# A long-convolution and gated-FFN kernel: the down projection is interleaved with the last iterations of the main loop

## The chip, the cores and the metric

The kernel runs on one core of a Trainium2 chip. The metric is the device time of one execution in microseconds. Before the change four runs took 963.98 to 967.84 us, median 966.01.

## The reference

The input `A_u` holds 2048 tokens with 576 channels. Each token is normalized. Three terms are added: the input, a state-space convolution of the normalized input, and a gated feed-forward network (FFN) of it.

```
xn = layernorm(u)                                   # 2048 x 576
K[d, l] = Re( sum_n C[d,n] * exp(dt[d]*A[d,n]*l) * dt[d]*B[d,n] )   # N = 128 states
y[l, d] = sum_{m<=l} K[d, l-m] * xn[m, d] + xn[l, d] * Dskip[d]
h       = relu(xn @ W_gate) * (xn @ W_up)           # 2048 x 4608
out     = u + y + h @ W_down
```

The FFN takes its input from the same normalized tokens; `B_x` is not read by the sum. The reference takes the convolution by FFT; the kernel computes it in blocks.

## The kernel before, in words

Each engine (PE, DVE, ACT, GpSimd, SP) has a list of instructions written out by one Python program, in program order. An engine runs its list strictly in that order; `wait` puts a wait for a semaphore count into it. All DMAs are issued by SP, so a wait in SP's list holds every DMA that is written after it.

After a setup (parameters, layer norm, transposed input `xnT`, reversed input `xnUr`), the main loop runs over iterations i = 0 to `NITER`. The 576 channels are taken four at a time, as 144 groups `sg` (`SGN`). The 2048 tokens are 16 chunks of 128. For a group the work is:

- G: powers of the state matrix, from a broadcast DMA of `muG` (L633), ACT's exponential and two sines (L651, L662, L663) and a DVE product (L677). This is done four to eight groups ahead, four groups in a block.
- R: eight matmuls of G with the reversed input (L693, L694), iteration i = sg. DVE copies the result (L711).
- E: eight transposes of G (L793) and a copy to a slot of `Ept` (L799); there are `NE` = `DY` + 1 slots.
- A scan over the 16 chunks on GpSimd, for eight groups at once (a batch, 18 in all): a memset (L730), 15 steps of three dependent operations (L738, L740, L742), then the products that make the right-hand sides of the cross term, ending with L774. It is written into GpSimd's list after the batch's last R.
- The cross term, which carries the state into each chunk, `DY` iterations after R (L833, L834): it needs E and the scan of its batch. DVE adds it to `xyev`, which gathers the output in SBUF (L845), and keeps a column of the convolution kernel K (L846).
- For each `KG` channels the K columns are transposed (L855), copied (L863) and written to DRAM by SP (`Kpad`, L866). From there a DMA builds Toeplitz matrices for two groups (L882), in one of three slots, and their matmuls (L898) come `DT` iterations after R. DVE adds the result to `xyev` (L908).

The FFN is cut into 288 units (128 hidden features by 256 tokens). A unit is ten matmuls (L976), a maximum (L989) and a product (L993) on DVE. SP stores two units of hidden states at a time to `hT_scr` in DRAM (L1017), from four slots; L993 of a unit waits for the store that frees its slot. `_ffn_w` gives a weight to each iteration, and the share of the weights up to i is the share of units that are out by then. Weight slabs come by DMA (L942, L945) for each 16 units.

At i = `SGN` + 10 SP waits for the last scan, among others, and loads all of W_down in four DMAs (L1063) over dead buffers. After the loop a second phase follows. SP waits for everything, then loads hidden states in blocks of 256 tokens, two slots (L1195). For each chunk of 128 tokens PE runs 36 pairs of matmuls (L1224, L1226). DVE adds the projection and the input (L1234, L1235) and then `xyev` (L1237) into a staging buffer, which SP stores (L1239) as soon as it is done.

In the order of one iteration, PE's list has R, the FFN units, the cross term, the K transpose, the E transposes and the Toeplitz matmuls; DVE's has the FFN steps, the copy of E, then the results of R, cross, K and Toeplitz.

Of the kernel before, what the change touches and what calls it, by code (L numbers as in the profile page):

```python
# [6 lines left out]
dt = mybir.dt  # L7
ACT = mybir.ActivationFunctionType
ALU = mybir.AluOpType

P = 128
# [116 lines left out]
def bass_parallel_sum__ssm_conv_s4__glu_gated_reglu__prompt_kernel(  # L128
# [16 lines left out]
    ctx = ExitStack()  # L145
    ctx.__enter__()

    L = A_u.shape[1]
    D = A_u.shape[2]
    N = A_A_re.shape[1]  # L150
    F = B_W_gate.shape[1]
    C = L // P
    KT = (D + P - 1) // P
    DR = [min(P, D - P * k) for k in range(KT)]
    FT = F // P
    assert L % P == 0 and N == P and F % 512 == 0 and D % 4 == 0 and D > 512

    SGN = D // 4
# [3 lines left out]
    NBATCH = D // SB  # L162
# [5 lines left out]
    NGM = BK + 2  # L168
    NT = 3
    NH = 4  # L170
    DY = 20
    NE = DY + 1
    KG = 32
    SG_PER_KG = KG // 4
    NKG = D // KG
    DT = DY + SG_PER_KG + 4
# [5 lines left out]
    NUNITS = NFB * FT_PER_FB * NTB  # L182
# [9 lines left out]
    sp = Eng("sync")  # L192
    act = Eng("scalar")
    pe = Eng("tensor")
    dve = Eng("vector")
# [85 lines left out]
    def Eslot(sg):  # L281
        t = Ept[sg % NE]
        return {"all": t, "r": t[:, 0, :, :], "i": t[:, 1, :, :]}
    Rsb = [A.tensor([SB, 2, C], dt.bfloat16) for _ in range(2)]
    Hst1 = A.tensor([SB, 2, C], dt.float32)
    Hst = [Hst1, Hst1]
# [20 lines left out]
    ph1_top = A.top  # L307

    A.top = ph0_base
    TB2 = 256  # L310
    NTB2 = L // TB2
    wd = A.tensor([FT, D], dt.bfloat16)
    assert A.top <= early_dead_top, (A.top, early_dead_top)
    hblk = [A.tensor([FT, TB2], dt.bfloat16) for _ in range(2)]
    xst = [A.tensor([D], dt.bfloat16) for _ in range(2)]
    acc32 = [A.tensor([D], dt.float32) for _ in range(2)]
    ost = [A.tensor([D], dt.bfloat16) for _ in range(2)]
    ph2_top = A.top
    print(f"[kern] arena: persistent={persistent_top} ph0_top={ph0_top} ph1_top={ph1_top} ph2_top={ph2_top} of {A.nbytes}")

# [517 lines left out]
    def emit_ycev(sg, bank, base, yg):  # L838
        d0, k, p0, r32 = sg_info(sg)
        dve.wait(tYCpe[sg], tokYevInit, ygrp["last_pe"][yg])  # L840
        pv = psf(bank, base, 68)
        in_y = bass.AP(tensor=pv.tensor, offset=pv.offset, ap=[pv.ap[0], [1, C], [17, 4]])
        out_y = xyev[:, :, d0:d0 + 4]
        in_k = bass.AP(tensor=pv.tensor, offset=pv.offset + C, ap=[pv.ap[0], [17, 4]])
        dve.op(lambda e: e.tensor_tensor(out_y, in_y, out_y, ALU.add), g_dve)  # L845
        tKcol[sg] = dve.op(lambda e: e.tensor_copy(Kall[:, d0:d0 + 4], in_k), g_dve)  # L846
        tYCev[sg] = tKcol[sg]
# [54 lines left out]
    def emit_yiev(sg, bank, base, yg):  # L902
        d0, k, p0, r32 = sg_info(sg)
        dve.wait(tYIpe[sg], tYCev[sg], ygrp["last_pe"][yg])
        pv = psf(bank, base, 64)
        in_y = bass.AP(tensor=pv.tensor, offset=pv.offset, ap=[pv.ap[0], [1, C], [C, 4]])
        out_y = xyev[:, :, d0:d0 + 4]
        tYIev[sg] = dve.op(lambda e: e.tensor_tensor(out_y, in_y, out_y, ALU.add), g_dve)  # L908

    def emit_ygroup_evacs(yg):  # L910
# [90 lines left out]
    def emit_hdma(u):  # L1001
# [18 lines left out]
        else:  # L1020
# [3 lines left out]
            if u2 is not None:  # L1024
# [3 lines left out]
                dst2 = hT_dram[ft2, :, TB * tb2:TB * tb2 + TB]  # L1028
                tHdma[u2] = sp.op(lambda e: e.dma_start(dst2, hst[u2 % NH][:, :]), g_hdma[u2 % NH], 16)

    def _ffn_w(i):
        if i < 40:
            return 1.35
        if i < SGN:
            return 1.0
        return 0.55
    _wtot = sum(_ffn_w(i) for i in range(NITER + 1))
    _wcum = []
    _acc = 0.0
# [9 lines left out]
    g_wd = [S(f"g_wd{q}") for q in range(4)]  # L1049
    tWd = []  # L1050

    def emit_wd_prefetch():
        sp.wait(tEcp[SGN - 1], tEtr[SGN - 1], tRev[SGN - 1], tZ[NBATCH - 1], tScan[NBATCH - 1],
                tGprod[SGN - 1], tGact[SGN - 1], tGmag[SGN - 1], tRpe[SGN - 1])
        for gi_ in range(NGB):
            sig = g_gbc[gi_]
            sp.wait((sig, sig.count))
        FT_PER = 9
        assert FT % FT_PER == 0
        for q in range(FT // FT_PER):  # L1060
            src = bass.AP(tensor=B_W_down.tensor, offset=B_W_down.offset + q * FT_PER * P * D,
                          ap=[[D, P], [P * D, FT_PER], [1, D]])
            tWd.append(sp.op(lambda e, q=q, src=src: e.dma_start(wd[:, FT_PER * q:FT_PER * (q + 1), :], src), g_wd[q], 16))  # L1063

    def emit_iteration_body(i):
        if i == SGN + 10:
            emit_wd_prefetch()
        if i < SGN:
            emit_R(i, i)
        target_units = int(round(NUNITS * _wcum[min(i, NITER)]))  # L1070
# [76 lines left out]
    assert len(tYIev) == SGN and len(tYCev) == SGN, (len(tYIev), len(tYCev))  # L1147
    assert len(tHdma) == NUNITS

    tokYev = tYIev[SGN - 1]  # L1150
    tokH = [tHdma[u] for u in range(NUNITS - NH, NUNITS)]
    tokPh1PE = tYIpe[SGN - 1]
    tokPh1PEf = tFFpe[NUNITS - 1]

    if STOP_AFTER == "phase1":
        finish_debug_phase1(locals())
        return

    emit_phase2(locals())


def emit_phase2(v):
    nc = v["nc"]
    sp, act, pe, dve, pool = v["sp"], v["act"], v["pe"], v["dve"], v["pool"]
    S = v["S"]
    P_, D, C, L, FT, KT, DR = P, v["D"], v["C"], v["L"], v["FT"], v["KT"], v["DR"]
    g_pe, g_dve, g_act = v["g_pe"], v["g_dve"], v["g_act"]
    psf = v["psf"]
    wd, hblk, xst, acc32, ost = v["wd"], v["hblk"], v["xst"], v["acc32"], v["ost"]
    hT_dram, B_W_down, x_pcd, out_pcd = v["hT_dram"], v["B_W_down"], v["x_pcd"], v["out_pcd"]  # L1170
    xyev = v["xyev"]
    TB2, NTB2 = v["TB2"], v["NTB2"]
    tHdma, NUNITS, NH = v["tHdma"], v["NUNITS"], v["NH"]
    tokYev, tokPh1PE, tokPh1PEf = v["tokYev"], v["tokPh1PE"], v["tokPh1PEf"]
    tFFev, tFFpe = v["tFFev"], v["tFFpe"]
    g_hdma = v["g_hdma"]

    tWd = v["tWd"]
    assert len(tWd) == 4, "wd prefetch not emitted"
    g_hb = [S("g_hb0"), S("g_hb1")]  # L1180
    g_xs = [S("g_xs0"), S("g_xs1")]
    g_out = [S("g_out0"), S("g_out1")]

    pe_last = tokPh1PE
    sp.wait(tokPh1PE, tokPh1PEf, tokYev, (v["g_act"], v["g_act"].count), (v["g_pool"], v["g_pool"].count),
            (g_dve, g_dve.count))
    for u in range(max(0, NUNITS - NH), NUNITS):
        sp.wait(tHdma[u])
    for s_ in range(NH):
        sig = g_hdma[s_]  # L1190
        sp.wait((sig, sig.count))
    def load_hblk(tb):
        s = tb % 2
        src = bass.AP(tensor=hT_dram, offset=TB2 * tb, ap=[[L, P], [P * L, FT], [1, TB2]])
        return sp.op(lambda e: e.dma_start(hblk[s][:, :, :], src), g_hb[s], 16)  # L1195

    def load_x(c):
        s = c % 2
        return sp.op(lambda e: e.dma_start(xst[s][:, :], x_pcd[:, c, :]), g_xs[s], 16)

    tHb = {}
    tXs = {}
    tHb[0] = load_hblk(0)
    if NTB2 > 1:
        tHb[1] = load_hblk(1)
    tXs[0] = load_x(0)
    tXs[1] = load_x(1)
    tDown = {}
    tComb = {}
    tOut = {}  # L1210
    B_D = [(0, 1), (2, 3)]
    pe.wait(*tWd)
    for tb in range(NTB2):
        s = tb % 2
        pe.wait(tHb[tb])
        for tt in range(TB2 // P):
            c = (TB2 // P) * tb + tt
            par = c % 2
            bA, bB = B_D[par]
            if c - 2 >= 0:  # L1220
                pe.wait(tComb[c - 2])
            for f in range(FT):
                lhsT = hblk[s][:, f, P * tt:P * tt + P]
                pe.op(lambda e, bA=bA, lhsT=lhsT, f=f: e.matmul(psf(bA, 0, 512), lhsT, wd[:, f, 0:512],  # L1224
                                                             start=(f == 0), stop=(f == FT - 1)), g_pe)
                t = pe.op(lambda e, bB=bB, lhsT=lhsT, f=f: e.matmul(psf(bB, 0, D - 512), lhsT, wd[:, f, 512:D],  # L1226
                                                                 start=(f == 0), stop=(f == FT - 1)), g_pe)
            tDown[c] = t
            ss = c % 2
            dve.wait(tDown[c], tXs[c], tokYev)  # L1230
            if c - 2 >= 0:
                dve.wait(tOut[c - 2])
            a32 = acc32[ss]
            ta = dve.op(lambda e, a32=a32, bA=bA, ss=ss: e.tensor_tensor(a32[:, 0:512], psf(bA, 0, 512), xst[ss][:, 0:512], ALU.add), g_dve)  # L1234
            tb_ = dve.op(lambda e, a32=a32, bB=bB, ss=ss: e.tensor_tensor(a32[:, 512:D], psf(bB, 0, D - 512), xst[ss][:, 512:D], ALU.add), g_dve)  # L1235
            dve.wait(ta, tb_)
            tComb[c] = dve.op(lambda e, a32=a32, ss=ss, c=c: e.tensor_tensor(ost[ss][:, :], a32[:, :], xyev[:, c, :], ALU.add), g_dve)  # L1237
            sp.wait(tComb[c])
            tOut[c] = sp.op(lambda e, c=c, ss=ss: e.dma_start(out_pcd[:, c, :], ost[ss][:, :]), g_out[ss], 16)  # L1239
            if c + 2 < C:  # L1240
                sp.wait(tComb[c])
                tXs[c + 2] = load_x(c + 2)
        if tb + 2 < NTB2:
            sp.wait(tDown[(TB2 // P) * tb + (TB2 // P) - 1])
            tHb[tb + 2] = load_hblk(tb + 2)
    finish(v["nc"], v["ctx"], [sp, act, pe, dve, pool], [(g, g.count) for g in g_out])


def finish(nc, ctx, engs, final_waits):
# [86 lines left out]
```

## Time and profile before

| | |
|---|---|
| median of four runs | 966.01 us |
| profiled execution, its own time | 965.23 us |
| its span, first to last instruction | 963.4 us |
| mean granted TensorE clock | 0.901 |
| PE busy | 676.2 us (70%) |
| DVE busy | 592.6 us (62%) |
| GpSimd busy | 498.1 us (52%) |
| ACT busy | 425.1 us (44%) |
| first R copy, last R copy | 156.2 us, 718.3 us |
| first scan, last scan begin | 182.2 us, 730.6 us |
| first matmul of the second phase | 816.1 us |

Busy shares are averages over stages with different limits: the second phase has PE alone, the main loop has all five engines. The small gaps between GpSimd's dependent steps are not counted as busy, though nothing else can run in them.

### The profile page before, as it was taken

To read this page: it belongs to the slowest core of one execution; us is meant where nothing else is said; L and a number is where in the kernel's file an instruction comes from. 1 tells how busy PE (TensorE), PEld (TensorE's weight loads), DVE (VectorE), ACT (ScalarE), POOL (GpSimd) and SP (SyncE) were. 2 spreads that over 40 slices of the span, in tenths; PEclk is the share of its full clock that TensorE was granted. 3 is DMA by queue.
4 is the path that set the end of the run, shared out by engine and by line. 5 is a ranking of instruction groups with operands and counts; after the bars stand their busy time and mean duration, and the time that the engine had idled before them with its cause. 6 is when DMAs were issued, how large, how long until landed. Compare 5 with 4: busy or idle time off the path is not lost.

```text
span 963.4 us, 21136 instructions
## 1 busy us (share of the span) xinstructions
PE 676.2 (70%) x8215; PEld 536.1 (56%) x8215; DVE 592.6 (62%) x1656; ACT 425.1 (44%) x602; POOL 498.1 (52%) x1004
## 2 busy tenths in 40 slices
PE   0040407887977967887878977887795164999998
PEld 0020306776866856776767866776684153555554
DVE  1639956886967967887878887888584042111111
ACT  0420149875846767678776767768400000000000
POOL 0000000388878788888888888888888400000000
PEclk9999967999989878988989887999898577999999
DMA  4000033544355455456665566464442467474760
GB/s 141 13 0 0 1 100 102 157 112 136 84 158 157 117 163 145 139 137 162 155 153 154 130 164 169 106 163 116 129 105 62 154 178 195 127 193 126 196 174 25
DMA packets 192195, 120.37 MB, mean 125 GB/s; under 512 B 86176, under 2 KB 173664, under 8 KB 192096
## 3 DMA queue, kind: packets, MB, share of 16 engines
q1 hardware_dynamic: 192096, 119.03, 46.6%
q8 instruction: 65, 1.06, 0.4%
q14 instruction: 34, 0.28, 0.1%
HBM read 97.17 MB, written 21.82 MB: 124 GB/s over the span
## 4 chain that ended last, share of the span: by engine, by line
PE 34%; DVE 20%; POOL 18%; DMA 15%; issue 5%; ACT 5%; SPq 4%; POOLq 0%; DVEq 0%; ACTq 0%
PE ps_all L976 14%; PE ps_all L1224 13%; DMA hT_scr<-arena 8%; POOL arena L738 5%; POOL arena L742 4%; DMA arena<-muG 3%; POOL arena L740 3%; DVE arena L799 3%; DVE arena L989 2%; DVE arena L993 2%; DVE arena L499 2%; DVE arena L677 2%; PE ps_all L793 2%; PE ps_all L1226 2%; DVE arena L528 2%
## 5 line engine op out<-in xcount | busy, mean ns | idle before, releaser
L976 PE MATMUL ps_all<-arena 128*128 128x256 bf16 x2880 | 381.7, 292 | 6.0 <-DVE arena L993 6.0
L976 PEld LDWEIGHTS ps_all<-arena 128*128 128x128 bf16 x2880 | 286.1, 104 | 53.6 <-DVE arena L993 6.5
L993 DVE TENSOR_TENSOR arena<-arena,ps_all 128x256 bf16<-128x256 bf16 x288 | 121.3, 421 | 110.9 <-DMA hT_scr<-arena 101.8
L651 ACT ACTIVATE arena<-arena 128x512 bf16<-128x512 bf16 x144 | 95.8, 714 | 156.4 <-DMA arena<-muG 140.7
L738 POOL TENSOR_TENSOR arena<-arena 128x128 f32<-128x128 f32 x270 | 145.5, 539 | 21.2
L1224 PE MATMUL ps_all<-arena 128*128 128x512 bf16 x576 | 143.3, 384 | 13.1 <-DMA arena<-hT_scr 13.1
L989 DVE TENSOR_SCALAR arena<-ps_all 128x256 bf16<-128x256 f32 x288 | 120.2, 418 | 29.2 <-PE ps_all L976 28.2
L693 PE MATMUL ps_all<-arena 128*128 128x16 bf16 x576 | 46.5, 170 | 106.2 <-DVE arena L908 64.7
L742 POOL TENSOR_TENSOR arena<-arena 128x64 f32<-128x64 f32 x270 | 106.0, 393 | 21.1
L662 ACT ACTIVATE arena<-arena 128x512 bf16<-128x512 bf16 x144 | 115.7, 803 | 0.5
L663 ACT ACTIVATE arena<-arena 128x512 bf16<-128x512 bf16 x144 | 115.2, 800 | 0.0
L1226 PE MATMUL ps_all<-arena 128*128 128x64 bf16 x576 | 111.6, 194 | 0.0
L740 POOL TENSOR_TENSOR arena<-arena 128x64 f32<-128x64 f32 x270 | 100.0, 370 | 21.2
L677 DVE TENSOR_TENSOR arena<-arena 128x2048 bf16<-128x2048 bf16 x72 | 97.5, 1354 | 17.2 <-ACT arena L663 17.2
L1224 PEld LDWEIGHTS ps_all<-arena 128*128 128x128 bf16 x576 | 56.7, 98 | 83.0 <-issue 15.9
L799 DVE COPY arena<-ps_all 128x1024 bf16<-128x1024 bf16 x144 | 98.5, 684 | 0.8 <-PE ps_all L898 0.7
L693 PEld LDWEIGHTS ps_all<-arena 128*128 128x128 bf16 x576 | 36.7, 97 | 110.1 <-DVE arena L908 67.5
L793 PE MATMUL ps_all<-arena 128*128 128x128 bf16 x1152 | 92.0, 225 | 0.0
L1234 DVE TENSOR_TENSOR arena<-ps_all,arena 128x512 f32<-128x512 f32 x16 | 11.1, 692 | 130.3 <-PE ps_all L1226 130.3
L793 PEld LDWEIGHTS ps_all<-arena 128*128 128x128 bf16 x1152 | 70.5, 100 | 1.6
L555 POOL MEMSET arena<- 128x32 bf16 x4 | 1.0, 418 | 130.5 <-DVE arena L528 130.5
L833 PE MATMUL ps_all<-arena 128*128 128x17 bf16 x576 | 47.6, 173 | 22.9 <-POOL arena L774 22.9
(111 smaller groups left out, 896.0 us busy)
## 6 DMA issues: line engine op xcount, KB each, us to landing
arena<-muG SPq DMA_DIRECT2D x72, 512.0 KB, 6.6
hT_scr<-arena SPq DMA_DIRECT2D x144, 128.0 KB, 2.7
arena<-Kpad SPq DMA_DIRECT2D x72, 256.0 KB, 4.9
arena<-hT_scr SPq DMA_DIRECT2D x8, 2304.0 KB, 10.6
arena<-in_B_W_down_dram SPq DMA_DIRECT2D x4, 1296.0 KB, 11.1
arena<-in_B_W_gate_dram SPq DMA_DIRECT2D x18, 256.0 KB, 5.2
arena<-in_B_W_up_dram SPq DMA_DIRECT2D x18, 256.0 KB, 4.1
arena<-in_A_u_dram SPq DMA_DIRECT2D x4, 576.0 KB, 5.7
```

The lines of the kernel that those rows point to most:

```text
L662: act.op(lambda e: e.activation(slot["r"][:, :, :], in_i, ACT.Sin, scale=cstc(C_JM), bias=cstc(C_PI2)), g_act)
L677: t = dve.op(lambda e: e.tensor_tensor(out, out, mag, ALU.mult), g_dve)
L738: t1 = eng.op(lambda e, Hrep=Hrep: e.tensor_tensor(sP4, Hrep, T4v4, ALU.mult), sig)
L740: t2 = eng.op(lambda e: e.tensor_tensor(sS, sPa, sPb, ALU.add), sig)
L742: tprev = eng.op(lambda e, Hn=Hn, Rp=Rp: e.tensor_tensor(Hn, sS, Rp, ALU.add), sig)
L793: t = pe.op(lambda e, o=o, part=part, j=j: e.transpose(o, gslot[part][:, j, :], identb[:, :]), g_pe)
L799: tEcp[sg] = dve.op(lambda e: e.tensor_copy(eslot["all"].ap.rearrange("p a b n -> p (a b n)"), psbf(bank, 0, 1024)), g_dve)
L976: t = pe.op(lambda e, o=o, lhsT=lhsT, rhs=rhs, k=k: e.matmul(o, lhsT, rhs, start=(k == 0), stop=(k == KT - 1)), g_pef)
L989: tFFact[u] = dve.op(lambda e: e.tensor_single_scalar(hr[:, :], psf(bank, 0, TB), 0.0, ALU.max), g_dve)
L993: tFFev[u] = dve.op(lambda e: e.tensor_tensor(hs[:, :], hr[:, :], psf(bank, TB, TB), ALU.mult), g_dve)
L1224: pe.op(lambda e, bA=bA, lhsT=lhsT, f=f: e.matmul(psf(bA, 0, 512), lhsT, wd[:, f, 0:512], start=(f == 0), stop=(f == FT - 1)), g_pe)
L1226: t = pe.op(lambda e, bB=bB, lhsT=lhsT, f=f: e.matmul(psf(bB, 0, D - 512), lhsT, wd[:, f, 512:D], start=(f == 0), stop=(f == FT - 1)), g_pe)
```

## The change

- `DY` goes from 20 to 17, `NE` follows (18 slots). `KG` goes from 32 to 16 channels, so there are 36 K groups; `DT` becomes 25 instead of 32 and `NITER` 169 instead of 176.
- The FFN weights become 1.3 for i < 40, 1.0 up to i = 146 (`FFN_END`), and 0 after it.
- W_down is laid only over the G buffers. Its four DMAs are issued at i = 144, 145, 146 and, in `p2_prepare`, at i = 147. They no longer wait for the scans.
- `p2_prepare` (i = 147) waits for all stores of hidden states and loads the first two blocks.
- From i = 151 (`P2_START`) each iteration begins with one chunk of the down projection (`p2_chunk`), before its cross and Toeplitz work. The blocks have 128 tokens and lie over `xnT`. The load for chunk c + 2 is issued after the addition of chunk c.
- The additions go into `xyev` in place, with DVE waits for its own earlier instructions around them and around the cross and Toeplitz additions. All 16 stores of the output are issued at the end.

```diff
-    DY = 20
+    DY = 17
     NE = DY + 1
-    KG = 32
+    KG = 16
...
-    TB2 = 256
+    TB2 = P
...
+        if p2_state["next"] > 0:
+            dve.wait((g_dve, g_dve.count))
         dve.op(lambda e: e.tensor_tensor(out_y, in_y, out_y, ALU.add), g_dve)
...
+    FFN_END = SGN + 2
     def _ffn_w(i):
         if i < 40:
-            return 1.35
-        if i < SGN:
+            return 1.3
+        if i <= FFN_END:
             return 1.0
-        return 0.55
+        return 0.0
...
-    def emit_wd_prefetch():
-        sp.wait(tEcp[SGN - 1], tEtr[SGN - 1], tRev[SGN - 1], tZ[NBATCH - 1], tScan[NBATCH - 1],
-                tGprod[SGN - 1], tGact[SGN - 1], tGmag[SGN - 1], tRpe[SGN - 1])
+    def emit_wd_prefetch(q):
+        sp.wait(tEtr[SGN - 1], tGprod[SGN - 1], tGact[SGN - 1], tGmag[SGN - 1], tRpe[SGN - 1])
...
+    P2_START = SGN + 7
+    def p2_prepare():
...
+        for s_ in range(NH):
+            sig = g_hdma[s_]
+            sp.wait((sig, sig.count))
+        sp.wait(tFFpe[NUNITS - 1])
+        p2_state["ready"] = True
+        p2_load(0)
+        emit_wd_prefetch(3)
+        p2_load(1)
+
+    def p2_load(c):
+        s_ = c % 2
+        if c - 2 >= 0:
+            sp.wait(tDown[c - 2])
+            sp.wait(tComb[c - 2])
+        src_h = bass.AP(tensor=hT_dram, offset=TB2 * c, ap=[[L, P], [P * L, FT], [1, TB2]])
+        tHb[c] = sp.op(lambda e: e.dma_start(hblk[s_][:, :, :], src_h), g_hb[s_], 16)
+        tXs[c] = sp.op(lambda e: e.dma_start(xst[s_][:, :], x_pcd[:, c, :]), g_xs[s_], 16)
+
+    def p2_chunk(c):
...
+        pe.wait(tHb[c])
...
+        if c - 2 >= 0:
+            pe.wait(tComb[c - 2])
+        for f in range(FT):
+            lhsT = hblk[s_][:, f, :]
+            pe.wait(tWd[f // 9])
...
+        dve.wait(tDown[c], tXs[c])
...
+        dve.wait(ta, tb_, (g_dve, g_dve.count))
+        tComb[c] = dve.op(lambda e, a32=a32, c=c: e.tensor_tensor(xyev[:, c, :], xyev[:, c, :], a32[:, :], ALU.add), g_dve)
+        if c + 2 < C:
+            p2_load(c + 2)
+
     def emit_iteration_body(i):
-        if i == SGN + 10:
-            emit_wd_prefetch()
+        if SGN <= i < SGN + 3:
+            emit_wd_prefetch(i - SGN)
+        if i == FFN_END + 1:
+            p2_prepare()
+        if i >= P2_START and p2_state["next"] < C:
+            p2_chunk(p2_state["next"])
+            p2_state["next"] += 1
...
+    sp.wait(tYIev[SGN - 1], tYCev[SGN - 1], (g_dve, g_dve.count))
+    for c in range(C):
+        sp.wait(tComb[c])
+        sp.op(lambda e, c=c: e.dma_start(out_pcd[:, c, :], xyev[:, c, :]), g_out[c % 2], 16)
```

More of the change, by code (lines that the diff above doesn't have):

```diff
@@ L283, in Eslot @@
         return {"all": t, "r": t[:, 0, :, :], "i": t[:, 1, :, :]}
+    g_dead_top = A.top
     Rsb = [A.tensor([SB, 2, C], dt.bfloat16) for _ in range(2)]
@@ L309, in bass_parallel_sum__ssm_conv_s4__glu_gated_reglu__prompt_kernel @@
     A.top = ph0_base
-    TB2 = 256
+    TB2 = P
     NTB2 = L // TB2
     wd = A.tensor([FT, D], dt.bfloat16)
-    assert A.top <= early_dead_top, (A.top, early_dead_top)
-    hblk = [A.tensor([FT, TB2], dt.bfloat16) for _ in range(2)]
+    assert A.top <= g_dead_top, (A.top, g_dead_top)
+    A.top = ph1_top
     xst = [A.tensor([D], dt.bfloat16) for _ in range(2)]
     acc32 = [A.tensor([D], dt.float32) for _ in range(2)]
-    ost = [A.tensor([D], dt.bfloat16) for _ in range(2)]
+    hblk_bytes = FT * TB2 * 2
+    assert 2 * hblk_bytes <= xnT.nbytes, (hblk_bytes, xnT.nbytes)
+    hblk = [Tens(A, xnT.boff + s_ * hblk_bytes, [FT, TB2], dt.bfloat16) for s_ in range(2)]
     ph2_top = A.top
@@ L907, in emit_yiev @@
         out_y = xyev[:, :, d0:d0 + 4]
+        if p2_state["next"] > 0:
+            dve.wait((g_dve, g_dve.count))
         tYIev[sg] = dve.op(lambda e: e.tensor_tensor(out_y, in_y, out_y, ALU.add), g_dve)
@@ L1058, in emit_wd_prefetch @@
         FT_PER = 9
-        assert FT % FT_PER == 0
-        for q in range(FT // FT_PER):
+        assert FT % FT_PER == 0 and len(tWd) == q
+        if True:
             src = bass.AP(tensor=B_W_down.tensor, offset=B_W_down.offset + q * FT_PER * P * D,
@@ L1063, in emit_wd_prefetch @@
             tWd.append(sp.op(lambda e, q=q, src=src: e.dma_start(wd[:, FT_PER * q:FT_PER * (q + 1), :], src), g_wd[q], 16))
-    def emit_iteration_body(i):
-        if i == SGN + 10:
-            emit_wd_prefetch()
+    g_hb = [S("g_hb0"), S("g_hb1")]
+    g_xs = [S("g_xs0"), S("g_xs1")]
+    tHb = {}
+    tXs = {}
+    tDown = {}
+    tComb = {}
+    P2_START = SGN + 7
+    p2_state = {"next": 0, "ready": False}
+    def p2_prepare():
+        assert unit_next[0] >= NUNITS, "all FFN units must be emitted before the down projection starts"
+        while pending_hdma:
+            emit_hdma(pending_hdma.pop(0))
+        for u_ in range(NUNITS):
+            assert u_ in tHdma, u_
+        for s_ in range(NH):
[6 more added lines that the diff above has]
+        p2_load(1)
@@ new lines, in p2_load @@
+    def p2_load(c):
[7 more added lines that the diff above has]
+    def p2_chunk(c):
+        s_ = c % 2
+        par = c % 2
+        bA = B_FF0 + 2 * par
+        bB = bA + 1
+        pe.wait(tHb[c])
+        if c < 2:
+            for u_ in range(max(0, NUNITS - NFFB), NUNITS):
+                pe.wait(tFFact[u_], tFFev[u_])
+        if c - 2 >= 0:
[3 more added lines that the diff above has]
+            pe.wait(tWd[f // 9])
+            pe.op(lambda e, bA=bA, lhsT=lhsT, f=f: e.matmul(psf(bA, 0, 512), lhsT, wd[:, f, 0:512],
+                                                         start=(f == 0), stop=(f == FT - 1)), g_pe)
+            t = pe.op(lambda e, bB=bB, lhsT=lhsT, f=f: e.matmul(psf(bB, 0, D - 512), lhsT, wd[:, f, 512:D],
+                                                             start=(f == 0), stop=(f == FT - 1)), g_pe)
+        tDown[c] = t
+        dve.wait(tDown[c], tXs[c])
+        a32 = acc32[s_]
+        ta = dve.op(lambda e, a32=a32, bA=bA, s_=s_: e.tensor_tensor(a32[:, 0:512], psf(bA, 0, 512), xst[s_][:, 0:512], ALU.add), g_dve)
+        tb_ = dve.op(lambda e, a32=a32, bB=bB, s_=s_: e.tensor_tensor(a32[:, 512:D], psf(bB, 0, D - 512), xst[s_][:, 512:D], ALU.add), g_dve)
+        dve.wait(ta, tb_, (g_dve, g_dve.count))
+        tComb[c] = dve.op(lambda e, a32=a32, c=c: e.tensor_tensor(xyev[:, c, :], xyev[:, c, :], a32[:, :], ALU.add), g_dve)
+        if c + 2 < C:
+            p2_load(c + 2)
@@ L1068, in emit_iteration_body @@
+    def emit_iteration_body(i):
+        if SGN <= i < SGN + 3:
[3 more added lines that the diff above has]
+        if i >= P2_START and p2_state["next"] < C:
+            assert p2_state["ready"]
+            p2_chunk(p2_state["next"])
+            p2_state["next"] += 1
         if i < SGN:
@@ L1148, in bass_parallel_sum__ssm_conv_s4__glu_gated_reglu__prompt_kernel @@
     assert len(tHdma) == NUNITS
[L1150 to L1153, printed above, removed]
+    if not p2_state["ready"]:
+        p2_prepare()
+    while p2_state["next"] < C:
+        p2_chunk(p2_state["next"])
+        p2_state["next"] += 1
+    g_out = [S("g_out0"), S("g_out1")]
+    sp.wait(tYIev[SGN - 1], tYCev[SGN - 1], (g_dve, g_dve.count))
+    for c in range(C):
+        sp.wait(tComb[c])
+        sp.op(lambda e, c=c: e.dma_start(out_pcd[:, c, :], xyev[:, c, :]), g_out[c % 2], 16)
     if STOP_AFTER == "phase1":
@@ L1157, in bass_parallel_sum__ssm_conv_s4__glu_gated_reglu__prompt_kernel @@
         return
[L1159 to L1246, printed above, removed]
@@ L1249, in finish @@
+    finish(nc, ctx, [sp, act, pe, dve, pool], [(g, g.count) for g in g_out])
 def finish(nc, ctx, engs, final_waits):
```

## The prediction

> **What bounds the kernel now.** I read the stretches of the span first, then GpSimd's waits, then SP's queue. Columns: stretch in us, its length, busy time (and count) of PE, weight loads, DVE, ACT, POOL, granted clock, DMA share, GB/s.
>
> ```profile
> 562.00:718.00 156.00, 122.64 (x1760) 108.04 (x1759) 122.87 (x354) 91.20 (x117) 135.57 (x267) 0.89 0.51 130
> 718.00:759.00 41.00, 18.72 (x269) 15.95 (x267) 15.30 (x66) 0.00 (x0) 35.28 (x74) 0.75 0.24 59
> 759.00:806.00 47.00, 27.96 (x325) 22.84 (x322) 19.74 (x74) 0.00 (x0) 0.00 (x0) 0.78 0.68 196
> 806.00:816.00 10.00, 0.00 (x0) 0.00 (x0) 0.00 (x0) 0.00 (x0) 0.00 (x0) 0.54 1.05 265
> 816.00:963.00 147.00, 143.33 (x1152) 73.37 (x1152) 25.31 (x48) 0.00 (x0) 0.00 (x0) 0.99 0.55 144
> ```
>
> From 816 the down projection runs alone with PE full: 16 chunks, 8.82 us apart (L1234 starts at 950.70 and 959.52). From 718 to 816, 98 us, PE works 47: it waits for the last scans, W_down, Toeplitz loads and hidden states. The loop before that is paced from two sides, by the scans on GpSimd (each begins with L730) and by the iterations, counted by DVE's copies of R (L711). Below: L730's own line, its waits from 182 to 349, and L711 alone in two stretches.
>
> ```profile
> L730 POOL MEMSET arena<- x18: 204/208/213, 182.2 to 730.6; 128x64 f32 x18
> POOL arena L730 <- DVE arena L711: 54.4, 4, 46.4
> 247.00:317.00 70.00, 4.49 (x16) 0.91 0.50 135
> 349.50:562.50 213.00, 15.73 (x56) 0.89 0.58 151
> ```
>
> Of the 54.4 us, 46.4 are the first batch's. GpSimd starved last at 349.5; a scan started there and at 541.6, six batches on, so 32.0 us each (over all 17 pitches, less 9.5 us of starving, 31.7). The iterations took 70/16 = 4.38 us in the dense FFN stage (i < 40) and 213/56 = 3.80 later, 30.4 for eight: there GpSimd is the pace. Scan 17 starts at 730.6, R 143 being done at 718.6.
>
> What disturbs the iterations is the store of hidden states. DVE waited for it eight times in those 213 us, about once for each group of 32 channels:
>
> ```profile
> DVE arena L993 <- DMA hT_scr<-arena: 29.8, 8, 4.8
> 459.44 0.32 SPq L866 DMA_DIRECT2D Kpad<-arena  x1
> 459.81 0.93 SPq L633 DMA_DIRECT2D arena<-muG  x2
> 460.87 0.38 SPq L882 DMA_DIRECT2D arena<-Kpad  x1
> 461.30 1.48 SPq L1017 DMA_DIRECT2D hT_scr<-arena  x1
> 462.87 1.83 SPq L882 DMA_DIRECT2D arena<-Kpad  x1
> 464.80 3.33 SPq L1017 DMA_DIRECT2D hT_scr<-arena  x1
> ```
>
> K's store, two G loads and two Toeplitz loads stand ahead of the last L1017 here; DVE got going again at 469.5.
>
> **The change, part by part.** *FFN pace.* By the weights, units per iteration go from 1.35 x 288/176.15 = 2.21 to 1.3 x 288/159 = 2.35 while i < 40, and from 1.635 to 1.811 later; at i = 143 283 of 288 are out instead of 258. Price of a unit: the two stages differ by 0.57 us and 0.57 units, so 1.0 us (DVE's own two steps are 421 + 418 ns; below that it can't go for long with DVE 80% busy). First stage: 94 units for 88, +6. Cross terms start 3 iterations and Toeplitz terms 7 earlier: 0.57 us of DVE (L845, L846, L908) at most in each, +2. So R 39, for which scan 4 waits until 316.3, moves to 324. Later, 3.80 + 0.18 = 3.98 us, 31.8 for eight: level with the scans, whose speed does not depend on FFN density (31.7 us for batches 3 and 4 with 2.2 units, 31.8 for 7 to 9 with 1.6).
>
> *Twice as many K groups.* 18 more transposes, DVE copies (0.2 us), stores of K (0.32 us of SP). PE waited 11.5 us before 18 transposes (L855), 0.64 each. Between nothing (GpSimd hides it) and 0.64 plus a store stall of 29.8/7 = 4.3 us, I take 0.3, near the transpose row, since the K store now falls an iteration after the two G loads, not just ahead of them: 13 groups, +4. R 143 is then at 324 + 104 x 3.98 + 4 = 742; the scans alone could not start batch 17 before 730.6 + 8 = 739.
>
> *DY 17.* PE now halts for scan b three iterations sooner, leaving 7 x 3.98 = 27.9 us of work under 31.8 of the next scan. The margin, 3.9 us, hides it; a longer disturbance would starve GpSimd, for its full excess in each of 13 batches. E has 18 slots for 21, freed one iteration ahead as before: nothing.
>
> *W_down moved to i = 144 to 147*, no longer behind the last scan. Four loads took 102% of the engines from 759 to 776, about 4 us each. On SP three of them now stand ahead of hidden-state stores and Toeplitz loads, and DVE's L993 queues behind those stores: iterations 144 to 146 at 6 us, not 4. Then SP drains the stores (3 us) and loads the first block. From R 143: 18 + 3 + 8 = 29, so chunk 0 starts at 771. Scan 17 ends at about 742 + 28 = 770, so iteration 153, which needs it, is not held.
>
> *Blocks of 128 tokens.* Runs in DRAM shrink from 512 to 256 bytes, 4608 of them per block either way.
>
> ```profile
> arena<-Kpad SPq DMA_DIRECT2D x72, 256.0 KB, 4.9
> arena<-hT_scr SPq DMA_DIRECT2D x8, 2304.0 KB, 10.6
> q1 hardware_dynamic: 5054, 2.79, 106.9%
> q1 hardware_dynamic: 1897, 0.57, 86.6%
> ```
>
> The two q1 lines are 839 to 849, nearly all 512-byte packets, and 781.3 to 784, nearly all 256-byte ones: 10 x 16 x 1.069/5054 = 34 ns and 2.7 x 16 x 0.866/1897 = 20 ns. A block is 288 packets on each of 16 engines: 5.7 us plus some 2 around it, 8. The Trainium skill (DMA: Bandwidth & Descriptors, Specifications) puts line rate at 512 bytes and more, with a read-modify-write below. Read as no gain from halving a packet, a block stays at 10.6. A load starts at the addition of chunk c (1.7 us after its last matmul, 959.52 to 961.20) and must land before chunk c+2. PE needs 0.6 (an iteration's 8 cross and 4 Toeplitz matmuls, 0.3 us each lot) + 8.82 + 0.6 = 10.0 from the end of c; the load 1.7 + 8 = 9.7. The chunks stay 9.5 apart, a shade above 9.4 for Toeplitz loads in the queue; by the rule, (8.82 + 1.7 + 10.6)/2 = 10.6. I take the row.
>
> *Chunks among the last iterations.* The 45 us of tail (759 to 804) hide under chunks as those 0.6 us. The 26 added DVE waits (9 cross, 17 Toeplitz steps from iteration 152 on) cost 0.11 each (L1235's end 960.33 to L1237's start 960.44), 2.9 us in all, under 9 us of PE each iteration. With that cover gone the 2.9 would be on the path. Chunk 0 starts with the clock low (816.1 to 827.9 is 11.8, not 8.8): +3. Chunks end at 771 + 152 + 3 = 926.
>
> *Stores of the output* all move behind the last addition: 926 + 0.5 + 1.7, then 16 x 8 packets per engine at 51 ns, 6.5, and 2.2 to land: span 937. The profiled execution was 965.23 with a span of 963.4, 1.8 apart, and the median is 966.01, so near that no correction is due. Predicted: 938, 3% less.
>
> **The rivals.** *Fast:* R gains stores better spread, so R 143 is done 12 us ahead of scan 17's start, as now: 739 - 12 + 29 = 756 for chunk 0, 15 earlier, and the sum ends at 923. For it: SP's burst is broken up. Against: every unit still costs DVE 0.84. *Blocks at the price of the rule:* 16 x 1.1 more, 956. For it: read and write sides differ between Kpad and hT_scr. *Slower:* the 4.3 us stall belongs to each K store, and comes every four iterations. Then 13 x 4.3 = 56 more on R, GpSimd starves each batch, and the end is at 994. For it: one stall per group, right behind L866. Against: the G loads come every four iterations already, and stall only where K's store and two Toeplitz loads join them. It decides against the change above 31/13 = 2.4 us per group. *The overlap does not come about:* chunk 0 would start near 816 only if an earlier PE instruction or the block load waited for the tail; ahead of it stand only iterations to 150, all fed by scan 16. So it is folded into the slower case, not a case of its own.
>
> **How the numbers follow.** Main case (926 to 950) 0.52; fast 0.12; rule's price 0.17; slower 0.16; a milder stall that ends within 0.3% of no change 0.03. A run of this kernel tells 0.3%, some 3 us, from nothing. Faster 0.52 + 0.12 + 0.17 = 0.81, same 0.03, slower 0.16. The range 914 to 968 leaves out the slower case and a little of the fast one.
>
> **What would show it.** Right: scan 17 starts at 739 to 745; the first down-projection matmul at 765 to 777; additions 9.3 to 9.8 us apart; last output store some 7 us behind the last addition. Wrong: GpSimd waiting for L711 in most batches after i = 40 (stall per group), the down-projection matmul waiting for hT_scr between chunks (rule's price), or PE idle between chunks for Toeplitz loads queued behind SP's waits for additions, which I price at nothing as they are issued three iterations ahead.

## The result and the profile after

The changed kernel takes 915.2 us (median of 10 runs, 913.48 to 916.0), 0.9476 of the kernel before (median 965.4 beside it), with a 95% interval of 0.9463 to 0.9489. The prediction was 938 with a range of 914 to 968. The direction was right and the size too small: 5.2% where 2.9% was forecast. The sum ended 25 us late; the case called fast in the rivals (span 923) came nearest. The result lies inside the range by 1.2 us only and outside the main case of 926 to 950, and what put it there is not something that the main sum counted on. The profiled execution's span is 912.1 us.

Line numbers move: L711 of before is L714 after, L730 is L733, L774 is L777, L866 is L871, L633 is L636, L882 is L887, L1017 is L1024, L993 is L1000, L833 is L836, L742 is L745, L1224 is L1119; L1234 is now the store of the output. First the stretches of the changed kernel, with the same columns as before (length, PE, weight loads, DVE, ACT, GpSimd, clock, DMA share, GB/s).

```profile
562.00:718.00 156.00, 126.96 (x1805) 112.60 (x1804) 122.23 (x365) 96.36 (x124) 135.79 (x264) 0.90 0.53 135
718.00:749.00 31.00, 16.06 (x216) 13.17 (x214) 12.73 (x53) 0.00 (x0) 26.42 (x60) 0.76 0.83 228
749.00:903.00 154.00, 149.59 (x1307) 78.49 (x1305) 32.63 (x89) 0.00 (x0) 9.70 (x16) 0.98 0.75 153
903.00:912.00 9.00, 0.00 (x0) 0.00 (x0) 0.00 (x0) 0.00 (x0) 0.00 (x0) 0.60 0.77 262
```

PE is full from 749 on, 67 us sooner than the 816 of before, and GpSimd is still at its last scan for the first 9.7 busy us of that stretch. The main loop is not shorter: the last scan starts at 731.6, where before had 730.6. What is new in the loop is who waits. These are GpSimd's starts and some waits, the first two lines of the whole run, the last two of 349 to 562 only.

```profile
L733 POOL MEMSET arena<- x18: 204/207/213, 184.5 to 731.6; 128x64 f32 x18
POOL arena L733 <- DVE arena L714: 53.7, 4, 47.6
PE ps_all L836 <- POOL arena L777: 19.1, 5, 5.2
DVE arena L1000 <- DMA hT_scr<-arena: 13.7, 12, 5.1
```

From 349 on GpSimd never waits for R. PE waits for GpSimd, 5 times and up to 5.2 us, so the scans alone set the pace, with 11% more FFN units in each iteration. DVE's wait for the store of hidden states is 13.7 us in this stretch, and was 29.8 before; over the whole run it is 45.7 us, and was 101.8. For each K group of the stretch that is 1.0 us (13.7 over 14 groups) where it was 4.3. That is the part the prediction did not have. SP's queue around one K store (L871) shows why it is worth asking about:

```profile
459.86 0.41 SPq L1024 DMA_DIRECT2D hT_scr<-arena  x1
462.22 0.32 SPq L871 DMA_DIRECT2D Kpad<-arena  x1
464.28 0.34 SPq L1024 DMA_DIRECT2D hT_scr<-arena  x1
467.51 0.37 SPq L887 DMA_DIRECT2D arena<-Kpad  x1
469.92 0.32 SPq L1024 DMA_DIRECT2D hT_scr<-arena  x1
470.33 0.39 SPq L887 DMA_DIRECT2D arena<-Kpad  x1
470.77 1.17 SPq L636 DMA_DIRECT2D arena<-muG  x2
```

Before, the two G loads (muG) came right behind the K store. Here they come 8 us after it, and each store of hidden states (L1024) in these lines is issued in 0.3 to 0.4 us, where one in the lines of before took 3.33.

### The profile page after: what moved, and what is told of

Read it like the earlier page. It is cut to its first block, busy times and chain, and to the rows that moved or that the text cites. A ratio compares the mean times of both kernels' runs of the same rounds, so it can differ in the third digit from the quotient of the medians.

```text
span 912.1 us, 21226 instructions
## 1 busy us (share of the span) xinstructions
PE 665.9 (73%) x8233; PEld 531.4 (58%) x8233; DVE 590.3 (65%) x1674; ACT 425.2 (47%) x602; POOL 500.1 (55%) x1004
## 4 chain that ended last, share of the span: by engine, by line
PE 31%; POOL 30%; DVE 15%; DMA 11%; issue 5%; ACT 5%; SPq 2%; POOLq 0%; DVEq 0%; ACTq 0%
PE ps_all L983 11%; PE ps_all L1119 11%; POOL arena L741 9%; POOL arena L745 6%; POOL arena L743 6%; DMA arena<-hT_scr 4%; DMA hT_scr<-arena 4%; DMA arena<-muG 3%; DVE arena L502 2%; PE ps_all L796 2%; DVE arena L531 2%; DVE arena L802 2%; POOL arena L769 2%; POOL arena L775 2%; PE ps_all L1121 1%
## 5 line engine op out<-in xcount | busy, mean ns | idle before, releaser
L983 PE MATMUL ps_all<-arena 128*128 128x256 bf16 x2880 | 362.1, 284 | 3.6 <-DVE arena L1000 3.6
L983 PEld LDWEIGHTS ps_all<-arena 128*128 128x128 bf16 x2880 | 281.0, 101 | 45.7 <-DVE arena L1000 4.7
L741 POOL TENSOR_TENSOR arena<-arena 128x128 f32<-128x128 f32 x270 | 158.3, 586 | 21.2
L1000 DVE TENSOR_TENSOR arena<-arena,ps_all 128x256 bf16<-128x256 bf16 x288 | 121.3, 421 | 54.6 <-DMA hT_scr<-arena 45.7
L1119 PE MATMUL ps_all<-arena 128*128 128x512 bf16 x576 | 146.2, 386 | 8.4 <-DMA arena<-hT_scr 8.4
L745 POOL TENSOR_TENSOR arena<-arena 128x64 f32<-128x64 f32 x270 | 101.8, 377 | 21.1
L680 DVE TENSOR_TENSOR arena<-arena 128x2048 bf16<-128x2048 bf16 x72 | 93.3, 1296 | 17.3 <-ACT arena L666 17.3
L1119 PEld LDWEIGHTS ps_all<-arena 128*128 128x128 bf16 x576 | 56.9, 99 | 77.3 <-DMA arena<-hT_scr 8.8
L836 PE MATMUL ps_all<-arena 128*128 128x17 bf16 x576 | 47.3, 173 | 50.2 <-POOL arena L777 49.4
L696 PEld LDWEIGHTS ps_all<-arena 128*128 128x128 bf16 x576 | 36.5, 96 | 71.6 <-DVE arena L915 32.7
L836 PEld LDWEIGHTS ps_all<-arena 128*128 128x128 bf16 x576 | 41.6, 97 | 56.4 <-POOL arena L777 47.4
```

Of the source, the lines that this page charges most:

```text
L741: t1 = eng.op(lambda e, Hrep=Hrep: e.tensor_tensor(sP4, Hrep, T4v4, ALU.mult), sig)
L745: tprev = eng.op(lambda e, Hn=Hn, Rp=Rp: e.tensor_tensor(Hn, sS, Rp, ALU.add), sig)
L983: t = pe.op(lambda e, o=o, lhsT=lhsT, rhs=rhs, k=k: e.matmul(o, lhsT, rhs, start=(k == 0), stop=(k == KT - 1)), g_pef)
L1000: tFFev[u] = dve.op(lambda e: e.tensor_tensor(hs[:, :], hr[:, :], psf(bank, TB, TB), ALU.mult), g_dve)
```

## The experiments

The open question: why did a loop with more FFN work and twice as many K groups wait less? Two causes were set against each other first, the grouping of K and the pace of the FFN.

**1. The changed kernel with K groups of 32.**

```diff
-    KG = 16
+    KG = 32
```

> The changed kernel with KG back at 32 (18 K groups; DT becomes 29, so four more iterations, about 1 us). Theory, K grouping: the store of hidden states was late because one K store, two G loads and two Toeplitz loads met on SP; groups of 16 channels break that up. Then DVE's wait for the store goes back from 46 us to 80 to 110, R 143 moves from 724 to 730 to 740, and the time is 922 to 932. Rival, the pace or DY did it: the wait stays at 40 to 55 us and the time within 3 us of 915.

Measured: 917.85 us, 0.950 of before (0.9468 to 0.9531). R 143 is done at 725.7, and DVE waits 59.2 us for the store. By the time and by R 143 that is the rival's outcome, though the wait is a little above its 40 to 55: the size of the groups is not the cause.

**2. The kernel before with K groups of 16.**

```diff
-    KG = 32
+    KG = 16
```

> The kernel before with KG 16 alone. K grouping: DVE's wait for the store falls from 102 us to about 50, iterations get shorter until the scans alone pace them, scan 17 still starts at 727 to 731, and the time gains only from the shorter tail (DT 28 for 32): 955 to 964. Rival: the wait stays near 100 us, time within 3 us of 966. The recorded prediction's doubled stall: wait near 150, time 980 or more.

Measured: 984.97 us, 1.0195 of before (1.0164 to 1.0225). DVE's wait for the store rises to 123.4 us over the whole run, and R 143 comes at 743.0 instead of 718.6. My theory was wrong in its sign. The prediction's slower rival was right in kind for this kernel: here twice as many K stores do cost more stalls. In the full change they do not. An iteration takes 4.17 us (between R 47 and R 103) where before has 3.80.

**3. The kernel before with the new FFN pace.**

```diff
-            return 1.35
-        if i < SGN:
+            return 1.3
+        if i <= SGN + 2:
             return 1.0
-        return 0.55
+        return 0.0
```

> The kernel before with the new FFN weights alone (1.3, 1.0 up to i = 146, then 0). At 1.0 us per unit, as the prediction priced it: R 39 at 322, R 143 at 736 to 742, scan 17 starts at 738 to 743, the tail loses its 12 or so units (10 us): 962 to 972. Rival, denser units cost little: R 143 within 5 us of 718.6, scan 17 at 730 to 733, 953 to 960.

Measured: 969.9 us, 1.0015 of before (0.9989 to 1.0041). R 39 at 321.3, R 143 at 733.9, 3.98 us per iteration. The price of 1.0 us per unit holds here to the last digit. But by the waits it is stall and not work: between R 47 and R 103 DVE waits 39.9 us for the store, 0.71 us per iteration, where before it waited 29.8 us, 0.53 per iteration. The wait grew by 0.18 us, and so did the iteration. So both costs of the prediction exist in the kernel before, this one as longer stalls, and something else in the change takes them away.

**4. The changed kernel without the interleaving.**

```diff
-    P2_START = SGN + 7
+    P2_START = NITER + 1
```

> The changed kernel with all 16 chunks behind the last iteration (P2_START past the end), everything else as it is. If the interleaving is what hides the tail: scan 17 ends at 760, the cross and Toeplitz tail without chunks takes some 25 us more, chunk 0 starts at about 785 instead of 749, 16 chunks at 8.8 us, end at 940 to 948. Rival, the early loads alone bring the gain: 915 to 922.

Measured: 945.11 us, 0.9781 of before (0.9755 to 0.9807). Chunk 0 starts at 784.2. The interleaving is worth 945.1 - 915.2 = 30 us; the rest of the change leaves 22.

**A new theory: where the K store falls.** What is left is DY. The K transpose of a group comes DY + 4 (KG 16) or DY + 8 (KG 32) iterations after the group's first R. With DY 20 that is iteration 0 modulo 4, with DY 17 iteration 1. The G loads are issued after each iteration 0 modulo 4. In SP's list the order between 350 and 660 us is K store, G load, G load in every case in the kernel before and in experiment 2, and in the changed kernel never so: a hidden-state store, a weight slab or a Toeplitz load follows. The theory: since SP waits at the K store for DVE's copy of the transpose, the G loads are held by that wait in the first order and are free in the second. Experiments 5 and 9 move the K work alone, by one iteration (and the Toeplitz matmuls, through DT); 6 and 7 change DY. Each of them moves the K transpose on PE and its copy on DVE together with the store on SP; no run moves the store alone.

**5. Experiment 2 with the K work one iteration later.**

```diff
-            if kg not in tKtr and last_sg_grp in tKcol:
+            if kg not in tKtr and last_sg_grp in tKcol and i % 4 == 1:
...
-    DT = DY + SG_PER_KG + 4
+    DT = DY + SG_PER_KG + 5
```

> The second experiment's kernel (before with KG 16, DY 20) with each K group's transpose, copy and store one iteration later (i mod 4 = 1, DT one more); nothing else. Theory, phase: with DY 20 the K store stands on SP right ahead of the two G loads that follow every fourth iteration (i mod 4 = 0), so SP sits in the wait for DVE's copy with G loads and hidden-state stores behind it; with DY 17 it falls at i mod 4 = 1. Then DVE's wait for the store falls from 123 us to 45 to 70, R 143 from 743 to 718 to 726, and the time from 985 to 958 to 968. Rival, DY's shorter lead itself: wait stays at 110 to 130, time 980 to 990.

Measured: 965.44 us, 0.9976 of before (0.9962 to 0.999), 19.5 us less than experiment 2. R 143 at 713.3, earlier than expected and than in any other run here. The wait for the store between 349 and 562 in experiment 2 and in this one:

```profile
DVE arena L993 <- DMA hT_scr<-arena: 34.8, 12, 6.8
DVE arena L993 <- DMA hT_scr<-arena: 6.3, 6, 1.6
```

Over the whole run it is 66.4 us, but 31.6 of them are a single wait in the tail, behind W_down. The loop is then paced by the scans, which do not get faster, so the time only returns to that of before.

**6. The changed kernel with DY 20.**

```diff
-    DY = 17
+    DY = 20
...
-    A.top = ph1_top
+    A.top = Wsl[0][0].boff
     xst = [A.tensor([D], dt.bfloat16) for _ in range(2)]
```

> The changed kernel with DY 20 (21 slots of E; the two addition buffers are laid over the weight slabs to make room). Phase back at i mod 4 = 0 with KG 16 and the dense pace: the wait for the store is 100 to 140 us, R 143 at 745 to 765, time 936 to 958. Rival, the block-wise down projection or anything else of the change made the loop faster: R 143 at 715 to 726, time 908 to 920.

Measured: 965.03 us, 0.998 of before (0.9957 to 1.0003). With DY put back, the whole gain is gone. (The second edit only lays two buffers elsewhere, to make room for 21 slots of E. Experiment 9 has that edit too and is fast.) The direction was expected, the size was more than expected: R 143 comes at 779.6. In its waits (349 to 562) and in SP's queue the old order is back:

```profile
DVE arena L1000 <- DMA hT_scr<-arena: 44.7, 12, 8.2
POOL arena L733 <- DVE arena L714: 29.3, 5, 7.6
471.42 0.32 SPq L871 DMA_DIRECT2D Kpad<-arena  x1
471.79 0.93 SPq L636 DMA_DIRECT2D arena<-muG  x2
472.76 0.47 SPq L1024 DMA_DIRECT2D hT_scr<-arena  x1
473.34 1.26 SPq L887 DMA_DIRECT2D arena<-Kpad  x1
474.70 2.76 SPq L1024 DMA_DIRECT2D hT_scr<-arena  x1
```

K store, both G loads, a store, a Toeplitz load, then a store that takes 2.76 us to issue. GpSimd now waits for R, five times in this stretch. An iteration takes 4.39 us between R 47 and R 103, where the changed kernel has 3.86.

**7. The changed kernel with DY 16.**

```diff
-    DY = 17
+    DY = 16
```

> The changed kernel with DY 16: shorter lead than 17, but the K store falls at i mod 4 = 0 as with 20. Phase: wait for the store 90 to 140 us, R 143 at 738 to 762, time 928 to 955. Rival, shorter lead: wait at or under 46 us, time 910 to 920.

Measured: 970.69 us, 1.0011 of before (0.9987 to 1.0035), R 143 at 784.3, wait for the store 127.5 us: the wait is as expected, the time and R 143 are later than that. DY 16 and DY 20 lie on both sides of 17 and share only the phase; both lose everything. It is not a shorter lead that helps.

**8. A version meant to beat both.** The dense first stage is taken out, and the output stores are spread over the last five chunks; the block of stores behind the last chunk goes.

```diff
-            return 1.3
+            return 1.0
...
-        if i >= P2_START and p2_state["next"] < C:
+        if i >= P2_START and p2_state["next"] < C and (i < P2_START + 2 or (i - P2_START) % 2 == 0):
...
+    stored = 0
     while p2_state["next"] < C:
-        p2_chunk(p2_state["next"])
+        cn = p2_state["next"]
+        p2_chunk(cn)
         p2_state["next"] += 1
+        sp.wait(tYIev[SGN - 1], tYCev[SGN - 1], tComb[cn])
+        for _ in range(4):
+            if stored <= cn:
+                sp.op(lambda e, c=stored: e.dma_start(out_pcd[:, c, :], xyev[:, c, :]), g_out[stored % 2], 16)
+                stored += 1
...
```

> A version that may beat both: FFN weights 1.0 for all i up to 146, and from iteration 153 on a chunk only every second iteration, the last five chunks behind the loop with the output stores spread between them. Flat pace: the first 40 iterations have 78 units for 94, so the scans alone pace from the start: R 39 at 311 or 312 for 317, scan 17 at 726, chunk 0 at 743 to 745. Stores: the last one 2 to 3 us behind the last addition instead of 10.7. Together 13 to 14 less: 900 to 904. If the later units cost more than the first ones save: 908 or more.

Measured: 903.8 us, 0.934 of before (0.9317 to 0.9363). R 39 comes at 304.9, sooner than expected, but R 143 only two us sooner than in the changed kernel, at 721.8: GpSimd now never waits after its first batch, and its 18 scans of 32 us are the floor. Most of the 11 us came from the stores. The last addition ends at 899.6 and the span at 901.8.

**9. Experiment 6 with the K work one iteration later.** The edit of experiment 5 on the kernel of experiment 6.

> The sixth experiment's kernel (the changed one with DY 20) with each K group's transpose, copy and store one iteration later, as in the fifth. Phase alone: the wait for the store falls from 132 us to 40 to 70, R 143 from 780 to 715 to 726, time from 965 to 908 to 920. If DY 17 has a gain of its own beside the phase: 925 or more.

Measured: 911.81 us, 0.9403 of before (0.9369 to 0.9436), 53 us less than experiment 6, R 143 at 723.5. Waits between 349 and 562:

```profile
DVE arena L714 <- POOL arena L745: 17.7, 5, 5.7
DVE arena L1000 <- DMA hT_scr<-arena: 12.9, 10, 3.8
```

DVE now waits for GpSimd, where it had waited 44.7 us for stores. SP's queue around one K store has a hidden-state store and a Toeplitz load behind it; the two G loads come at 484.68:

```profile
477.15 0.33 SPq L871 DMA_DIRECT2D Kpad<-arena  x1
477.52 0.42 SPq L1024 DMA_DIRECT2D hT_scr<-arena  x1
478.55 0.37 SPq L887 DMA_DIRECT2D arena<-Kpad  x1
```

With DY 20 and the order changed the gain is whole: DY 17 helped through the phase, and through nothing else that these runs can see.

**10. Versions 8 and 9 together** (DY 20 with the later K work, flat pace, chunks in iterations 151, 152 and every second one from 157, five behind the loop with up to five stores each).

> The eighth experiment's version with DY 20 and the later K store; chunks at iterations 151, 152, then every second one from 157, five behind the loop. R need not halt for a scan until three iterations later: R 143 at 714 to 719 for 722, chunk 0 at 740 to 744, time 897 to 901. Rival, the last scan now gates iteration 156 and costs what R gains: 902 to 908.

Measured: 901.62 us, 0.9312 of before (0.9291 to 0.9333), the fastest here. R 143 is done at 715.7, as hoped, and chunk 0 starts at about 739. The additions of chunks 1 and 2 are 15 us apart, since iterations 153 to 156 have no chunk: PE ended chunk 1 at 759.7 and began chunk 2 at 764.5. The rival did not come about there, as the last scan had ended at 759.5, before PE asked for it. The time lies between the two ranges, and the distance to version 8 (ratio intervals that overlap) is not decided.

## Why the prediction was right or wrong, point by point

**What bounds the loop: right.** GpSimd's scans were named as the pace after iteration 40, and they were, since GpSimd never waited for R from 349 on. The floor for the last scan, 739, was 7 us too late: it took over the 8 us that R 39 was to lose, and R 39 lost 1.0 (317.2 for 316.2), as did the last scan (731.6 for 730.6).

**The step that missed: DY 17 costed at nothing, with the 4.3 us stall kept inside the iteration.** R 143 was forecast for 742 and came at 723.9; 18 of the 25 us are here. The step weighed DY by the lead of R over the scans. That lead did shrink as described: PE waits for scans 11 times in 18 batches, 4.5 us each. But DY also sets the iteration of the K store, and so the order on SP. The text noted that the K store now falls an iteration apart from the G loads, and took from it only that the new K stores would add little. The stall of 29.8/7 us per group that it had measured stood in the 3.80 us per iteration, and the same edit took most of it away. Experiments 5, 6, 7 and 9 show it: the phase of the K work alone is worth 53 us on the changed kernel and 20 on experiment 2. The fast rival, given 0.12, named the right kind of reason (a burst on SP broken up) without saying which edit would do it.

**1.0 us per FFN unit: right where it was measured, wrong where it was used.** Experiment 3 has 3.98 us per iteration, as forecast, but the added 0.18 us are longer waits for the store and not DVE's own steps. In the changed kernel, where that stall is mostly gone, the extra units cost R 39 1 us, 317.2 for the forecast 324.

**0.3 us per K group: too low for the old order, too high for the new.** In the old order the denser groups cost 0.37 us per iteration (4.17 for 3.80), some 3 us per added group, ten times the 0.3; this is the slower rival's mechanism, and it was in the kernel all along. It decides in experiment 6, where it meets the dense pace: R 143 at 779.6, 38 us beyond the forecast for the change. In the new order groups of 16 and of 32 stand within 3 us of each other.

**W_down at i = 144 to 147: right, a little dear.** From R 143 to chunk 0 took 748.7 - 723.9 = 24.8 us for 29. Iterations 144 to 146 ended at about 738, 14 us after R 143, for 18.

**Blocks of 128 tokens: right.** The prediction priced a block by the row of traced packets and not by the rule, and the load time bears it out; the two lines are from the changed kernel, columns as before.

```profile
arena<-hT_scr SPq DMA_DIRECT2D x16, 1152.0 KB, 7.2
PE ps_all L1119 <- DMA arena<-hT_scr: 8.4, 5, 6.8
```

A block with half the bytes in as many packets lands in 7.2 us, not in 10.6. PE waits 8.4 us for blocks in all, 6.8 of them before chunk 0. Chunks start 9.47 us apart ((890.7 - 748.7)/15), forecast 9.5. The rival with the rule's price (chunks 10.6 apart) is out.

**Tail under the chunks: right.** No Toeplitz load was late enough to matter. Experiment 4 prices the cover that the prediction spoke of: without it the time is 30 us longer.

**Output stores: right kind, 2 us short.** From the last addition's end to the end of the span are 912.1 - 901.4 = 10.7 us for 8.7. In the profile of the changed kernel SP issues them in one piece:

```profile
902.42 7.76 SPq L1234 DMA_DIRECT2D out_dram<-arena  x16
```

SP took 0.49 us per store, where the 6.5 us of the sum were packet time.

Of the signs of being right, two came early (scan 17 at 731.6 for 739 to 745, the first down-projection matmul at 748.7 for 765 to 777), while the additions were 9.3 us apart, as said. None of the signs of being wrong came. The sum was right to within 5 us in each later step; with R 143 at 723.9 in place of 742 it would have ended at 919.

## What to carry to other kernels

When one queue issues all DMAs and also waits, look at the order of its list before counting its work: in experiment 6 an 8 KB store stood right ahead of two 512 KB loads, and moving its work by one iteration gave 53 us. A lookahead constant does two things, it sets how far one stage runs ahead and, modulo the period of another stage, which instructions stand next to each other; cost both. When a stall recurs once per group, ask for each edit whether the stall survives it, before carrying the measured time per iteration over.

## What was not expected of the hardware

Moving the K work by one iteration, with the same work on every engine and the same bytes, was worth 53 us of 965 (experiments 6 and 9). The traces of these two narrow down how, between 349 and 562 us. The first three lines are of experiment 6, the others of experiment 9; the last number of a DMA line is the median time from issue to landing.

```profile
ACT arena L654 <- DMA arena<-muG: 82.9, 24, 7.6
hT_scr<-arena SPq DMA_DIRECT2D x43, 128.0 KB, 4.5
arena<-Kpad SPq DMA_DIRECT2D x24, 256.0 KB, 7.8
ACT arena L654 <- DMA arena<-muG: 37.8, 20, 4.4
hT_scr<-arena SPq DMA_DIRECT2D x50, 128.0 KB, 3.0
arena<-Kpad SPq DMA_DIRECT2D x28, 256.0 KB, 3.8
```

G loads did come late, but only ACT waited for them; neither DVE nor PE waited for ACT or for G in this stretch, so late G did not hold the loop by itself. What held it was DVE's wait for the hidden-state stores, and these took longer after they were issued. SP did not wait less at the K store in the fast order: 45.7 us at 13 stores in experiment 9, 36.9 us at 12 in experiment 6. So the length of that wait is not what makes the fast order fast. That the G and Toeplitz loads ahead of a 128 KB store delay its landing fits these lines, but no run moves them alone. The K transposes and copies moved too: PE waited 8.1 us for K columns (L860) in this stretch of experiment 6, and not at all in experiment 9. That share is not separated.

GpSimd's first 16 scans took 30.0 to 34.1 us in all these runs, and the last two 28 to 30, when ACT and DVE had less to do. Denser FFN work did not slow them visibly: their mean is 31.8 us in the kernel before and in experiment 3, and 31.9 in the changed kernel. The stalled experiment 6 has 31.2, experiment 9 without those stalls 32.3; why is open.
